# GpSimd takes the clamps of the first layer and eight scalings, two row tiles for the scatter, and new ranks

## The chip, the cores and the metric

The kernel runs on one core of a Trainium2 chip, as one program. The metric is the device time of an execution in microseconds (us), and of several executions the median. A core has five engines that each work through a list of instructions of their own, in the order in which the program was built, and wait for each other by semaphores: TensorE (PE: matrix products; PEld is its loading of weights), VectorE (DVE), ScalarE (ACT), GpSimd (POOL) and SyncE (SP, which here only starts transfers).

## The reference: what is computed

Three parts in a row, over B = 2 batches of S = 576 tokens (T = 1152 tokens), with 8 heads of 64 columns, so 512 columns a token:

```python
scores = q @ k.T / sqrt(64)                    # each batch and head: 576 x 576
kth    = the 32nd largest score of each row    # scores under it are masked
attn   = exp(scores - max); attn /= attn.sum() + 1e-9
x      = attn @ v                              # all heads of a token side by side: 512 columns
h      = x @ w_in                              # 512 -> 2048
x      = (h * cos(h)) @ w_out                  # 2048 -> 512
e      = argmax(x @ w_gate)                    # one of 8 experts for each token
gate   = softmax(x @ w_gate)[e]
out    = gate * relu(x_slot @ w1[e]) @ w2[e]   # 512 -> 1024 -> 512, at most 288 tokens an expert
```

w_in and w_out come as 64-bit floats and are turned into 32-bit floats on the chip.

## The kernel before

**Attention.** There are 36 steps; a step holds 2 x 128 rows of 576 scores (two heads of one tile of 128 tokens). `scores` makes them on PE (L482) and ACT copies them out of PSUM into `Sp` (L494). DVE finds the 32nd largest value in `pair_chain`: it takes the larger and then the smaller of the two halves of each row (L509, 128x576 in one instruction) and runs lists of maxima over them (MAX8, L513, L522, L524, and MATCH_REPLACE8, L517). `softmax` then makes the penalty on ACT (L556), subtracts it on POOL (L559), takes the exponential on ACT (L561) and divides each row by its sum: a multiplication by the reciprocal `sm`, on ACT (L570) for the first `na` steps and on DVE (L574) for the others. `products` turns the probabilities over on PE (L589), copies them on ACT (L591) and multiplies by v on PE (L603, L605; L616, L618), into `av`.

**The 2048-wide layer.** Nine tiles of 128 tokens are taken one alone and then in four pairs. `layer_in` makes 128x512 of h per unit (four tokens' blocks of w_in columns for the lone tile, two for a pair): three products of rounded halves for a pair (L684 to L686), a copy on ACT (L691) into `hs`, and a clamp of the angle into `ur` (L695, a minimum and a maximum with two constants, 36 of them for the whole kernel). `cosine` is on ACT (L712), where a switch between the exponential and the sine loads a table; `product` is on POOL (L720) and `layer_out` on PE (L729), into `x2`. `w_in` and `w_out` are converted first: `convert` makes each of 32 weight tiles of 128x512 with ACT, DVE and POOL (L389 to L408), `split_w` rounds w_in (`wh`, L365) and subtracts (`wl`, L359).

**Routing and experts.** `route` copies a tile's 128 rows into the row tile `xr` (L742), turns them over (L660, L744), makes the logits (L748) and picks the expert with small DVE instructions (L751 to L761); `place` counts the place in the expert (L786, L789 to L792) and POOL scatters the rows of `xr` to `xs` in DRAM by an indirect transfer (L795). There is one `xr`. When all nine tiles are scattered, SP reads the rows back by expert (`xg`, L953 to L957), and eight experts follow, each a first layer (L979, L981) and a second (L1010).

**What sets the order.** Every operation is entered into `Plan` with an engine, a cost and a rank. `emit` walks through time with these costs: of the operations that an engine could start within 0.02 us of its earliest, it takes the one of lowest rank. It gives buffers as they come free. The order of each engine's list thus comes out of the costs, the ranks and the rings of buffers. The parameters of the ranks and of the division of work stand in `PRM`; `FULL` is for a second pass that these inputs don't take.

```python
PRM = dict(na=22, mul=1, c0=-4.505, c1=0.411, c2=-30.35, ...)
            if s < prm["na"]:                               # scaling of step s: on ACT, else on DVE
    ring("xr", "mx", [128, RW], F32)                        # the row tile: one buffer
            P.op("dve", 0.34, lambda: DVE.tensor_scalar(angle(), T[kh], QUARTER, -QUARTER, op0=OP.min, op1=OP.max),
```

Of the kernel before, what the change touches and what calls it, by code (L numbers as in the profile page):

```python
# [7 lines left out]
F32 = mybir.dt.float32  # L8
# [4 lines left out]
AF = mybir.ActivationFunctionType  # L13
OP = mybir.AluOpType
# [3 lines left out]
B, H, S, D = 2, 8, 576, 64  # L18
HS = S // 2
T = B * S  # L20
# [5 lines left out]
RW = 520  # L26
# [14 lines left out]
QUARTER = 1.5707  # L41
FEWER = 1023.4


PRM = dict(na=22, mul=1, c0=-4.505, c1=0.411, c2=-30.35, c3=1.14, sm=-6.538, pr=0.274, sc=2.931, mx=-1.055, co=1.204, lo=5.261, ro=7.18, tb=9.729, ga=4.016, lod=10, pc=0, lv=11.745, sw=6.214, s1=0.597)
FULL = dict(na=12, mul=8, c0=3.627, c1=-2.562, c2=3.854, c3=0.425, sm=1.002, pr=3.858, sc=5.283, mx=0.736, co=8.685, lo=1.174, ro=7.507, tb=11.194, ga=4.52, lod=4, pc=0, lv=2.808, sw=1.416, s1=0.894)


class Plan:
# [202 lines left out]
def forward(ctx, lasting, tc, kq, vn, vs_, w_in, w_out, w_gate, w1, w2, out, paired):  # L252
# [3 lines left out]
    P = Plan(prm["tb"])  # L256
# [14 lines left out]
    def ring(name, pool, shape, dtype, bufs=1, tag=None, gate=None):  # L271
        P.ring(name, lambda: pools[pool], shape, dtype, bufs, tag, gate)
# [97 lines left out]
    def convert(n):  # L370

        kt = (("wt", "wt3", "wt2", "wt", "wt3", "wt2")[n % 6], n)
        kr = ("wraw2" if n % 3 else "wraw", n)
        kf = slot_of(n)
        if n < 16:
            u, kc = divmod(n, 4)
            src, r0, c0 = w_in, kc * 128, u * 512
        else:
            src, r0, c0 = w_out, (n - 16) * 128, 0

        def full():
            return T[kf] if n < 16 else T["wo", 0][:, n - 16, :]

        def bits(t):
            return t.bitcast(I32)

        last = P.dma(0.45, 1.65, lambda: SP.dma_start(
            T[kr], src[r0:r0 + 128, 2 * c0:2 * c0 + 1024].rearrange("p (n t) -> p n t", t=2)), w=[kr])
        P.op("act", 0.56, lambda: ACT.activation(T[kt], T[kr][:, :, 1].bitcast(F32), AF.Copy, scale=2.0 ** -112),  # L389
             r=[kr], w=[kt])  # L390
        if n < prm["mul"]:

            P.op("dve", 0.34, port=True, fn=lambda: DVE.tensor_scalar(bits(full()), bits(T[kt]), 3, None,
                                                                      op0=OP.logical_shift_left), r=[kt], w=[kf])
            P.op("dve", 0.60, port=True, fn=lambda: DVE.scalar_tensor_tensor(
                bits(full()), T[kr][:, :, 0], 29, bits(full()), op0=OP.logical_shift_right, op1=OP.bitwise_or),
                r=[kr], w=[kf])
            P.op("dve", 0.60, port=True, fn=lambda: DVE.scalar_tensor_tensor(
                bits(full()), bits(T[kt]), SIGN, bits(full()), op0=OP.bitwise_and, op1=OP.bitwise_or),
                r=[kt], w=[kf])  # L400
        else:
            P.op("act", 0.56, lambda: ACT.activation(full(), T[kr][:, :, 1].bitcast(F32), AF.Sign), r=[kr], w=[kf])
            P.op("dve", 0.34, port=True, fn=lambda: DVE.tensor_scalar(bits(T[kt]), bits(T[kt]), 3, None,
                                                                      op0=OP.logical_shift_left), w=[kt])
            P.op("dve", 0.60, port=True, fn=lambda: DVE.scalar_tensor_tensor(  # L405
                bits(T[kt]), T[kr][:, :, 0], 29, bits(T[kt]), op0=OP.logical_shift_right,
                op1=OP.bitwise_or), r=[kr], w=[kt])
            P.op("pool", 1.27, lambda: POOL.tensor_tensor(out=full(), in0=T[kt], in1=full(), op=OP.mult), r=[kt],  # L408
                 w=[kf])
        return last  # L410
# [133 lines left out]
    def softmax(s):  # L544
        both = [("W", s, 0), ("W", s, 1)]

        def scalars():
            w = T["W", s]
            POOL.tensor_tensor(out=T["tb", s], in0=w[:, :, TH:49:48 - TH], in1=factors[:, None, :].to_broadcast([128, 2, 2]),  # L549
                               op=OP.mult)  # L550
            if paired:
                POOL.tensor_tensor(out=edge[:, s], in0=w[:, :, 39], in1=w[:, :, TH], op=OP.subtract)
        P.op("pool", 0.3, scalars, r=both + [("halfpi",)], w=[("edge", s), ("tb", s)])
        for i in range(2):
            ks, kp = ("Sp", s, i), ("pen", (s, i))
            P.op("act", 0.67, lambda i=i, kp=kp: ACT.activation(T[kp], T["Sp", s][:, i, :], AF.Relu, scale=-BIG,  # L556
                                                                bias=T["tb", s][:, i, 0:1]), r=[ks, ("tb", s)], w=[kp])

            P.op("pool", 1.34, lambda i=i, kp=kp: POOL.tensor_tensor(  # L559
                out=T["Sp", s][:, i, :], in0=T["Sp", s][:, i, :], in1=T[kp], op=OP.subtract), r=[kp], w=[ks])  # L560
            P.op("act", 0.76, lambda i=i: ACT.activation(  # L561
                T["Sp", s][:, i, :], T["Sp", s][:, i, :], AF.Exp, bias=T["tb", s][:, i, 1:2],
                accum_out=T["sm", s][:, i:i + 1]), r=[("tb", s)], w=[ks, ("sm", s, i)], table="exp")
        P.op("pool", 0.25, lambda: POOL.tensor_scalar(T["sm", s][:, 2:4], T["sm", s][:, 0:2], 1e-9, 1.0, op0=OP.add,
                                                      op1=OP.mult), r=[("sm", s, 0), ("sm", s, 1)], w=[("sm", s, 2)])
        P.op("dve", 0.08, lambda: DVE.reciprocal(T["sm", s][:, 0:2], T["sm", s][:, 2:4]), r=[("sm", s, 2)],
             w=[("sm", s, 3)])
        for i in range(2):
            if s < prm["na"]:
                P.op("act", 0.67, lambda i=i: ACT.activation(T["Sp", s][:, i, :], T["Sp", s][:, i, :], AF.Copy,  # L570
                                                             scale=T["sm", s][:, i:i + 1]),
                     r=[("sm", s, 3)], w=[("Sp", s, i)])
                continue
            P.op("dve", 0.39, lambda i=i: DVE.tensor_scalar(T["Sp", s][:, i, :], T["Sp", s][:, i, :],  # L574
                                                            T["sm", s][:, i:i + 1], None, op0=OP.mult),
                 r=[("sm", s, 3)], w=[("Sp", s, i)], port=True)
# [75 lines left out]
    ring("ur", "mx", [128, 2, 512], F32, 2, tag="ur")  # L652
    ring("nn", "mx", [128, 512], F32)
    ring("gT", "mx", [128, 512], F32)
    ring("xr", "mx", [128, RW], F32)
    ring("xr4", "mx", [128, RW], F32, tag="raw")

    def transposes(kp, src):
# [3 lines left out]
    def layer_in(t, u):  # L662
# [29 lines left out]
        def angle():  # L692
            return T["ur", (t, u // 2)][:, u % 2]
        if paired:
            P.op("dve", 0.34, lambda: DVE.tensor_scalar(angle(), T[kh], QUARTER, -QUARTER, op0=OP.min, op1=OP.max),  # L695
                 r=[kh], w=[ku], port=True)
            return
        P.op("pool", 0.59, lambda: POOL.tensor_scalar(angle(), T[kh], INV_2PI, 0.25, op0=OP.mult, op1=OP.add), r=[kh],
             w=[ku])
# [437 lines left out]
```

## Time and profile before

| | us |
|---|---|
| median of 3 runs | 698.27 (697.89 to 698.58) |
| the profiled execution | 697.17 |
| its span, first to last instruction | 695.4 |

The span falls into three stretches. Up to about 411 us DVE works through the lists of the 36 steps. From there to 501 us PE does what is left of the 2048-wide layer. From 501 to 530 us the last two tiles are routed and read back, and from 530 us on the experts run. A row of a profile gives busy time; the time between instructions on an engine that another engine sets costs nothing by itself, so each stretch is read by the engine that has no gaps in it. The records of one engine overlap a little where instructions follow closely.

### The profile page before, as it was taken

The page shows a single profiled execution, that of the slowest core. Times are in us where ns is not written, and L with a number is a line of the kernel's source. Part 1 is how long each engine was busy: PE and PEld are TensorE (multiplying, and loading weights), DVE is VectorE, ACT ScalarE, POOL GpSimd, SP SyncE. Part 2 cuts the span into 40 slices and gives each one's busy share as a digit, 9 for nine tenths or more (in the row PEclk, how much of TensorE's full clock was granted, in tenths as well). Part 3 has the DMA queues.
Part 4 walks back from the last instruction along what each step waited for, and adds up shares of the span by engine and source line. Part 5 has one row for each costly group of instructions (what it writes and reads, how often), then busy time and mean ns, then how long its engine had stood idle before and what let it go on. Part 6 is the DMA issues. An engine that isn't in the chain of part 4 may idle for free.

```text
span 695.4 us, 11074 instructions
## 1 busy us (share of the span) xinstructions
PE 587.0 (84%) x3611; PEld 431.9 (62%) x3611; DVE 552.0 (79%) x1654; ACT 494.3 (71%) x1004; POOL 265.8 (38%) x316
## 2 busy tenths in 40 slices
PE   3333577799999999989999899999926999999994
PEld 1122355545776755866756567667425888999993
DVE  5999999999999999999999962555223888889630
ACT  4676998999799989787877764566313777778631
POOL 3466675677445545464544541322110101101111
PEclk9995658999899999999999999999956999999997
DMA  9543552064131201000000002353113677787300
GB/s 348 189 151 124 163 168 92 1 231 182 56 101 39 71 6 39 20 16 17 1 1 1 0 17 87 126 169 135 61 46 123 224 250 251 266 269 259 108 18 16
DMA packets 30786, 77.28 MB, mean 111 GB/s; under 512 B 4606, under 2 KB 4606, under 8 KB 30720
## 3 DMA queue, kind: packets, MB, share of 16 engines
q1 hardware_dynamic: 28976, 71.73, 30.7%
q0 software_dynamic: 1744, 4.76, 1.8%
q8 instruction: 30, 0.49, 0.3%
q14 instruction: 36, 0.29, 0.1%
HBM read 64.57 MB, written 12.69 MB: 111 GB/s over the span
## 4 chain that ended last, share of the span: by engine, by line
PE 40%; DVE 35%; ACT 15%; DMA 3%; issue 3%; POOL 1%; SPq 1%; POOLq 0%; DVEq 0%; ACTq 0%
PE yp L1010 11%; DVE W L513 9%; DVE C L517 8%; PE x L729 8%; PE hp L979 7%; DVE C L509 5%; PE hp L981 3%; ACT Sp L561 2%; DVE W L522 2%; ACT pen L556 2%; DVE wt L405 2%; ACT Sp L570 2%; ACT Sp L494 2%; PE h L684 2%; DVE Sp L574 2%
## 5 line engine op out<-in xcount | busy, mean ns | idle before, releaser
L729 PE MATMUL x<-wo,hs 128*128 128x512 f32 x288 | 138.2, 603 | 0.0
L559 POOL TENSOR_TENSOR Sp<-Sp,pen 128x576 f32<-128x576 f32 x72 | 98.9, 1373 | 63.9 <-ACT pen L556 63.3
L513 DVE MAX8 W<-C 128x8 f32<-128x288 f32 x288 | 118.2, 446 | 0.6
L946 DVE TENSOR_TENSOR wl<-raw,wh 128x512 fp32r<-128x512 f32 x128 | 89.9, 739 | 35.4 <-ACT wh L944 34.9
L517 DVE MATCH_REPLACE8 C<-W,C 128x288 f32<-128x288 f32 x216 | 93.8, 440 | 0.0
L589 PE MATMUL pt<-ident,Sp 128*128 128x128 f32 x324 | 56.4, 304 | 39.1 <-ACT Sp L570 32.5
L482 PE MATMUL S<-kq 64*128 64x288 f32 x256 | 57.8, 533 | 28.7 <-ACT Sp L494 19.8
L589 PEld LDWEIGHTS pt<-ident,Sp 128*128 128x128 f32 x324 | 40.0, 153 | 66.9 <-ACT Sp L570 42.1
L944 ACT ACTIVATE wh<-raw 128x512 fp32r<-128x512 f32 x128 | 74.0, 621 | 9.9 <-DMA raw<-in_w_dram 6.9
L684 PE MATMUL h<-xh,wh 128*128 128x256 f32 x256 | 78.1, 305 | 0.5 <-ACT hs L691 0.4
L979 PE MATMUL hp<-xgs,wh 128*128 128x384 f32 x256 | 76.3, 368 | 0.0
L729 PEld LDWEIGHTS x<-wo,hs 128*128 128x128 f32 x288 | 49.0, 190 | 43.5 <-issue 42.7
L1016 POOL DMA_INDIRECT out_dram<-ot,ti x16 | 16.6, 1035 | 152.8 <-ACT ot L1025 121.6
L685 PE MATMUL h<-xl,wh 128*128 128x256 f32 x256 | 71.9, 281 | 0.0
L686 PE MATMUL h<-xh,wl 128*128 128x256 f32 x256 | 71.8, 281 | 0.0
L1010 PE MATMUL yp<-wh,hc 128*128 128x512 f32 x192 | 68.4, 400 | 0.0
L509 DVE TENSOR_TENSOR C<-Sp 128x576 f32<-128x576 f32 x72 | 65.1, 904 | 3.0 <-ACT Sp L494 2.2
L720 POOL TENSOR_TENSOR hs<-hs,ur 128x512 f32<-128x512 f32 x36 | 48.4, 1356 | 46.4 <-ACT ur L712 45.0
L561 ACT ACTIVATE Sp<-Sp,tb 128x576 f32<-128x576 f32 x72 | 55.6, 773 | 14.2 <-POOL Sp L559 14.0
L981 PE MATMUL hp<-xgs,wl 128*128 128x192 f32 x256 | 65.3, 255 | 0.0
L556 ACT ACTIVATE pen<-Sp,tb 128x576 bf16<-128x576 f32 x72 | 55.2, 767 | 6.3 <-POOL tb L549 5.5
L591 ACT ACTIVATE PT<-pt 128x384 f32<-128x384 f32 x108 | 48.6, 483 | 12.2 <-PE pt L589 12.0
(138 smaller groups left out, 1365.8 us busy)
## 6 DMA issues: line engine op xcount, KB each, us to landing
raw<-in_w_dram SPq DMA_DIRECT2D x64, 512.0 KB, 3.8
wraw<-in_w_out_dram SPq DMA_DIRECT2D x16, 512.0 KB, 3.8
wraw<-in_w_in_dram SPq DMA_DIRECT2D x16, 512.0 KB, 4.0
xs<-z SPq DMA_DIRECT2D x1, 4680.0 KB
kq<-in_kq_dram SPq DMA_DIRECT2D x8, 576.0 KB, 5.7
v<-in_vn_dram SPq DMA_DIRECT2D x8, 320.0 KB, 6.2
v<-in_vs_dram SPq DMA_DIRECT2D x8, 320.0 KB, 3.3
out_dram<-z SPq DMA_DIRECT2D x1, 2304.0 KB
```

Of the source, the lines that this page charges most:

```text
L509: DVE.tensor_tensor(out=T["C", s], in0=x[:, :, 0:HS], in1=x[:, :, HS:S], op=op)
L513: P.op("dve", 0.365, lambda r=r, i=i: DVE.max(T["W", s][:, i, LIST[r]:LIST[r] + 8], T["C", s][:, i, :]), r=[("C", s, i)], w=[("W", s, i)])
L517: P.op("dve", 0.42, lambda r=r, i=i: DVE.match_replace(T["C", s][:, i, :], T["W", s][:, i, LIST[r]:LIST[r] + 8], T["C", s][:, i, :], NEG), ...
L559: P.op("pool", 1.34, lambda i=i, kp=kp: POOL.tensor_tensor(out=T["Sp", s][:, i, :], in0=T["Sp", s][:, i, :], in1=T[kp], op=OP.subtract), r ...
L589: PE.transpose(T[kp][:, c * 128:(c + 1) * 128], P2[:, cc * 128:(cc + 1) * 128], ident)
L684: PE.matmul(o, hi, a, start=(kc == 0), stop=False, skip_group_check=True)
L729: P.op("pe", 0.86, lambda f=f, a=a: PE.matmul(T["x2", t], T[kh][:, a:a + 128], T["wo", 0][:, f, :], start=(f == 0), stop=(f == 15)), r=[kh ...
L944: P.op("act", 0.52, lambda a=a, hi=hi: ACT.activation(T[hi], T[kr][:, a * 512:(a + 1) * 512], AF.Copy), r=[kr], w=[hi])
L946: P.op("dve", 0.6, lambda a=a, hi=hi, lo=lo: DVE.tensor_tensor(out=T[lo], in0=T[kr][:, a * 512:(a + 1) * 512], in1=T[hi], op=OP.subtract), ...
L979: PE.matmul(T[kp][:, 0:2 * MAIN], T[ka][:, c:c + 128], x.rearrange("p a n -> p (a n)"), start=(kc == 0), stop=False, skip_group_check=True)
L981: PE.matmul(T[kp][:, 0:MAIN], T[kb][:, c:c + 128], x[:, 0], start=False, stop=(kc == 3), skip_group_check=True)
L1010: PE.matmul(T[kp], x, w, start=(fc + n == 0), stop=(fc == 7 and n == len(uses) - 1))
```

## The change

- **Clamps.** `layer_in` puts the clamp on POOL for the first `cl` tiles in their order. With `cl=16` these are all: 36 TENSOR_SCALAR of 128x512 go from DVE to POOL.
- **Scalings of probabilities.** `na` goes from 22 to 32: steps 22 to 31 move from DVE to ACT (20 instructions). The next `np=10` steps, of which there are four (32 to 35), go to POOL as a product of `Sp` and the reciprocal spread over the row (8 TENSOR_TENSOR of 128x576). DVE has none of its 28 left.
- **Row tiles.** `xr` gets a second buffer.
- **Weights.** `mul` goes from 1 to 3: two more tiles of w_in are put together by three DVE instructions, where before DVE had two, ACT took a sign and POOL multiplied. `lod` 10 to 16: all 16 subtractions of `split_w` are on DVE (six were on POOL). `pc` 0 to 8: eight of the 16 roundings go from ACT to POOL.
- **Ranks.** All numbers of `PRM` are new, so the order of every engine differs. w_in is now converted from its last tile to its first and ahead of the last five tiles of w_out; SP's list changes in the same way (the 16 loads of w_in and the last five of w_out trade places), the rest of it is the same. ACT's list has 27 table loads, before 31. `ts=0` leaves a new branch in `convert` unused.

```diff
-PRM = dict(na=22, mul=1, c0=-4.505, c1=0.411, c2=-30.35, c3=1.14, sm=-6.538, pr=0.274, sc=2.931, mx=-1.055, co=1.204, lo=5.261, ...
+PRM = dict(np=10, cl=16, ts=0, na=32, mul=3, c0=-6.12, c1=-0.119, c2=-35.561, c3=2.753, sm=-13.198, pr=-0.47, sc=3.501, ...
...
@@ softmax
+            if s < prm["na"] + prm["np"]:
+                P.op("pool", 1.34, lambda i=i: POOL.tensor_tensor(
+                    out=T["Sp", s][:, i, :], in0=T["Sp", s][:, i, :],
+                    in1=T["sm", s][:, i:i + 1].to_broadcast([128, S]), op=OP.mult), r=[("sm", s, 3)], w=[("Sp", s, i)])
+                continue
...
-    ring("xr", "mx", [128, RW], F32)
+    ring("xr", "mx", [128, RW], F32, 2)
...
@@ layer_in
-            P.op("dve", 0.34, lambda: DVE.tensor_scalar(angle(), T[kh], QUARTER, -QUARTER, op0=OP.min, op1=OP.max),
-                 r=[kh], w=[ku], port=True)
+            on_pool = order.index(t) < prm["cl"]
+            P.op("pool" if on_pool else "dve", 0.59 if on_pool else 0.34, lambda: (POOL if on_pool else DVE).tensor_scalar(
+                angle(), T[kh], QUARTER, -QUARTER, op0=OP.min, op1=OP.max), r=[kh], w=[ku], port=True)
```

Three places in the order. First DVE's list at the end of step 25's chain and the start of the next (`Sp` scaled by `sm`, `ur` the clamped angle, `C` and `W` the lists). Before:

```order
L517 MATCH_REPLACE C<-W,C 128x288 x2
L634 TENSOR_TENSOR xl<-av,xh 64x2x64 x2
L513 MAX W<-C 128x8 x2
L509 TENSOR_TENSOR C<-Sp 128x576
L522 MAX W<-C 128x8
L566 RECIPROCAL sm<-sm 128x2
L522 MAX W<-C 128x8
L574 TENSOR_SCALAR Sp<-Sp,sm 128x576 x2
L524 MAX W<-W 128x8 x2
L509 TENSOR_TENSOR C<-Sp 128x576
L695 TENSOR_SCALAR ur<-hs 128x512
```

The same place in the list of the changed kernel, in which lines stand up to ten further down:

```order
L517 MAX W<-C 128x8 x2
L513 TENSOR_TENSOR C<-Sp 128x576
L526 MAX W<-C 128x8 x2
L570 RECIPROCAL sm<-sm 128x2
L528 MAX W<-W 128x8 x2
L513 TENSOR_TENSOR C<-Sp 128x576
L517 MAX W<-C 128x8 x2
```

The two scalings and the clamp are gone from it; the chain itself is the same.

Second ACT's list in the same stretch of the changed kernel (`pen` the penalty, `PT` the copied probabilities):

```order
L565 ACTIVATE Sp,sm<-Sp,tb 128x576
L498 ACTIVATE Sp<-S 128x2x288
L574 ACTIVATE Sp<-Sp,sm 128x576 x2
L700 ACTIVATE hs<-h 128x512
L560 ACTIVATE pen<-Sp,tb 128x576
L650 ACTIVATE xh<-av 128x128
L722 ACT_TABLE_LOAD
L722 ACTIVATE ur,turns<-ur,halfpi 128x1024
```

Each step from 22 to 31 has such a pair of scalings (L574) here, which in the list before end with step 21.

Third ACT's list at the last two tiles, with the buffers' numbers (`xr` the row tile, `gT` the rows turned over, `small` the exponentials of the logits). Before, and below it after:

```order
L742 ACTIVATE xr_4963<-x2_4675 128x512
L744 ACTIVATE gT_4969<-pt_4968 128x512
L768 ACTIVATE small_87<-small_87 128x8
L742 ACTIVATE xr_5005<-x2_4754 128x512
L744 ACTIVATE gT_5010<-pt_5009 128x512
L768 ACTIVATE small_87<-small_87 128x8
L967 ACTIVATE xgs_5107<-xp_5101 128x192
```

```order
L752 ACTIVATE xr_4961<-x2_4667 128x512
L752 ACTIVATE xr_4972<-x2_4745 128x512
L754 ACTIVATE gT_4967<-pt_4966 128x512
L754 ACTIVATE gT_4989<-pt_4988 128x512
L778 ACTIVATE small_87<-small_87 128x8 x2
L977 ACTIVATE xgs_5105<-xp_5099 128x192
```

The two tiles' copies stood one whole routing apart; now they stand next to each other, and so do their later steps.

On PE, behind the last product of step 35 with v, the list before still has 3 x 72 products of `layer_in` and 53 of `layer_out`; the changed list has 3 x 80 and 56.

## Rows read from the trace of the kernel before

**Rows 1.** Windows: stretch, its length, busy time and count of each engine, clock, transfers.
```profile
70.00:105.00 35.00, 23.71 (x132) 17.28 (x133) 34.58 (x86) 33.84 (x67) 24.93 (x23) 0.65 0.51 163
140.00:268.00 128.00, 122.61 (x822) 79.69 (x818) 123.04 (x398) 117.11 (x224) 72.61 (x88) 0.97 0.27 94
268.00:374.00 106.00, 102.27 (x709) 70.35 (x707) 103.67 (x336) 82.71 (x161) 49.95 (x66) 1.00 0.05 15
374.00:411.00 37.00, 33.68 (x228) 24.85 (x228) 35.83 (x124) 26.24 (x51) 17.74 (x26) 1.00 0.03 9
411.00:501.00 90.00, 89.73 (x473) 58.31 (x472) 38.81 (x84) 49.31 (x87) 23.50 (x24) 1.00 0.33 112
501.00:530.00 29.00, 9.04 (x69) 6.84 (x68) 5.78 (x41) 3.54 (x10) 3.21 (x5) 0.55 0.28 94
530.00:695.00 165.00, 156.34 (x889) 141.06 (x888) 113.12 (x331) 106.56 (x269) 16.56 (x16) 0.97 0.53 176
```
**Rows 2.** Timeline of DVE and PE: ends of chains 22, 32, 35; last product with v.
```profile
267.67 0.30 DVE L524 MAX8 W<-W 128x8 f32<-128x16 f32 x2
...
374.06 0.23 DVE L524 MAX8 W<-W 128x8 f32<-128x16 f32 x2
...
410.41 0.24 DVE L524 MAX8 W<-W 128x8 f32<-128x16 f32 x2
...
425.50 0.27 PE L605 MATMUL av<-PT,v 128*64 128x128 f32 x1
```
**Rows 3.** Groups by line and shape: busy us, mean ns, idle before and its releasers.
```profile
L559 POOL TENSOR_TENSOR Sp<-Sp,pen 128x576 f32<-128x576 f32 x72 | 98.9, 1373 | 63.9 <-ACT pen L556 63.3 <-DVE wt L403 0.3
L509 DVE TENSOR_TENSOR C<-Sp 128x576 f32<-128x576 f32 x72 | 65.1, 904 | 3.0 <-ACT Sp L494 2.2
L570 ACT ACTIVATE Sp<-Sp,sm 128x576 f32<-128x576 f32 x44 | 31.6, 767 | 9.3 <-DVE sm L566 9.2
L405 DVE SCALAR_TENSOR_TENSOR wt<-wraw,wt 128x512 int32<-128x512 int32 x31 | 22.4, 735 | 0.1
L695 DVE TENSOR_SCALAR ur<-hs 128x512 f32<-128x512 f32 x36 | 20.0, 555 | 6.8 <-ACT hs L691 6.7
L574 DVE TENSOR_SCALAR Sp<-Sp,sm 128x576 f32<-128x576 f32 x28 | 15.4, 591 | 0.0
L755 DVE TENSOR_SCALAR onehot<-iota,small 128x8 bf16<-128x8 f32 x9 | 5.3, 586 | 0.3
L359 DVE TENSOR_TENSOR wl<-ws,wh 128x512 fp32r<-128x512 f32 x10 | 7.8, 787 | 0.0
L334 POOL MEMSET z<- 128x520 f32 x1 | 0.5, 532 | 0.0
```
**Rows 4.** Source view of two DVE lines: shortest, median and longest in ns.
```profile
L695 DVE TENSOR_SCALAR ur<-hs x36: 407/422/1808, 127.1 to 488.2; 128x512 f32<-128x512 f32 x36
L509 DVE TENSOR_TENSOR C<-Sp x72: 736/751/1861, 12.8 to 407.5; 128x576 f32<-128x576 f32 x72
```
**Rows 5.** Timeline of PE: two products of the first layer, 21 starts apart.
```profile
427.74 0.28 PE L685 MATMUL h<-xl,wh 128*128 128x256 f32 x1
...
430.25 0.28 PE L685 MATMUL h<-xl,wh 128*128 128x256 f32 x1
```
**Rows 6.** The chain that ended last: start us, us, what.
```profile
413.52 1.72 PE x L729 x4
...
506.76 2.81 DMA xs<-xr,slot
...
512.18 1.89 PE av L748 x8
...
517.41 4.03 DMA xs<-xr,slot x2
```
**Rows 7.** Timeline of ACT and PE at the last two tiles.
```profile
502.35 1.06 PE L748 MATMUL av<-wg,gT 128*128 128x8 f32 x8 [0.75 <-ACT gT L744]
...
509.67 0.60 ACT L742 ACTIVATE xr<-x 128x512 f32<-128x512 f32 x1 [4.78 <-DMA xs<-xr,slot]
```

More of the change, by code (lines that the diff above doesn't have):

```diff
@@ L42 @@
 FEWER = 1023.4
-PRM = dict(na=22, mul=1, c0=-4.505, c1=0.411, c2=-30.35, c3=1.14, sm=-6.538, pr=0.274, sc=2.931, mx=-1.055, co=1.204, lo=5.261, ro=7.18, tb=9.729, ga=4.016, lod=10, pc=0, lv=11.745, sw=6.214, s1=0.597)
-FULL = dict(na=12, mul=8, c0=3.627, c1=-2.562, c2=3.854, c3=0.425, sm=1.002, pr=3.858, sc=5.283, mx=0.736, co=8.685, lo=1.174, ro=7.507, tb=11.194, ga=4.52, lod=4, pc=0, lv=2.808, sw=1.416, s1=0.894)
+PRM = dict(np=10, cl=16, ts=0, na=32, mul=3, c0=-6.12, c1=-0.119, c2=-35.561, c3=2.753, sm=-13.198, pr=-0.47, sc=3.501, mx=-2.942, co=16.076, lo=16.671, ro=8.401, tb=47.632, ga=7.38, lod=16, pc=8, lv=15.338, sw=11.123, s1=2.383)
+FULL = dict(np=4, cl=2, ts=0, na=12, mul=8, c0=3.627, c1=-2.562, c2=3.854, c3=0.425, sm=1.002, pr=3.858, sc=5.283, mx=0.736, co=8.685, lo=1.174, ro=7.507, tb=11.194, ga=4.52, lod=4, pc=0, lv=2.808, sw=1.416, s1=0.894)
 class Plan:
@@ L388, in convert @@
             T[kr], src[r0:r0 + 128, 2 * c0:2 * c0 + 1024].rearrange("p (n t) -> p n t", t=2)), w=[kr])
-        P.op("act", 0.56, lambda: ACT.activation(T[kt], T[kr][:, :, 1].bitcast(F32), AF.Copy, scale=2.0 ** -112),
-             r=[kr], w=[kt])
+        if n < prm["ts"]:
+            P.op("pool", 0.7, lambda: POOL.tensor_scalar(T[kt], T[kr][:, :, 1].bitcast(F32), 2.0 ** -112, 0.0, op0=OP.mult,
+                                                         op1=OP.add), r=[kr], w=[kt])
+        else:
+            P.op("act", 0.56, lambda: ACT.activation(T[kt], T[kr][:, :, 1].bitcast(F32), AF.Copy, scale=2.0 ** -112),
+                 r=[kr], w=[kt])
         if n < prm["mul"]:
```

## The prediction

> **What bounds the kernel now.** I read the windows first, with their edges put at the ends of chains, then the timeline at those edges, then the groups by line, and last the chain of waits at the end. In the windows one looks for the engine without gaps: DVE has 123.04 of 128 us from 140 to 268 us, 103.67 of 106 from 268 to 374 and 35.83 of 37 from 374 to 411 [rows 1]. So up to 411 us the pace is DVE's, and the edges are the ends of the chains of steps 22, 32 and 35 [rows 2]. From 411 to 501 us PE has 89.73 of 90 us and DVE 38.81 [rows 1]: the 2048-wide layer has fallen behind, and PE works it off. PE is nearly full before that too, 102.27 of 106 and 33.68 of 37 us, which limits what a faster DVE can give. From 501 to 530 us no engine is busy; there the chain of waits goes from one tile's scatter to the next tile's logits and scatter [rows 6]. From 530 us PE has 156.34 of 165 us [rows 1]. The work of the experts is not changed but for some earlier transposes, and I leave it at zero; what hides these is that expert 0's and 1's weights are loaded well ahead in both lists.
>
> **Step 1, up to chain 22 (268 us): nothing.** DVE loses 12 clamps of 0.555 us (-6.7), gains six subtractions of 0.787 (+4.7) and a third instruction for two weights, priced as its like on L405, 2 x 0.735 (+1.5) [rows 3]. That is -0.5 us. The conversions stand in another order, but up to chain 10 and again up to chain 22 their number is about the same; a misplaced weight is two DVE instructions, so I allow 3 us either way. ACT loses eight roundings here, which is no gain where DVE sets the pace. The moved loads of w_in and w_out are queued on SP as before, ahead of nothing that is late.
>
> **Step 2, chains 23 to 32 (106 us): -4 us.** DVE loses 18 scalings of 0.591 and nine clamps of 0.555: 10.6 + 5.0 = 15.6 us [rows 3], which would leave it 88. But ACT takes 20 scalings of 0.767, 15.3 us [rows 3], on top of its 82.7: 98.0 us of work [rows 1]. ACT becomes the bound. With no gap at all it needs 98 us (-8); at the share it has from 140 to 268 us, 117.11 of 128 or 91.5%, it needs 107 (+1); at the fullest stretch of the trace, 33.84 of 35 or 96.7%, 101.4 [rows 1]. I take 102, near the last, since ACT would now be what the others wait for, as it nearly was there. What queues behind a scaling on ACT are the copies of scores that DVE's next chain needs.
>
> **Step 3, chains 33 to 35 (37 us): -7 us.** DVE loses eight scalings (4.7), four clamps (2.2) and the one-hot comparisons of two route picks that now stand behind chain 35 (2 x 0.586, with small neighbours not counted) [rows 3]: 8.1 us, so 27.7 of work. ACT gets no scaling here, and has 26.24 of 37. POOL gets them: eight products, bounded by its other two-input instruction of that shape, 1.373 [rows 3], so 11.0 on top of 17.74 [rows 1]. That is 28.7; with waits I take 30.
>
> **Clamps on POOL.** The trace has no such instruction on POOL. The nearest rows are a memset of 128x520 at 0.532 and the two-input 1.373 [rows 3]; I take 0.6, since a clamp reads one tensor, not two. 36 of them are 22 to 49 us on an engine that has gaps in every stretch (49.95 of 106, 23.50 of 90 [rows 1]), so they lie beside other work. The cover is gone if POOL stands in line behind a penalty that ACT is late with: L559 waited 63.3 us for ACT in all [rows 3], and a clamp behind it waits with it, then the cosine and PE's L729. Units wait in four buffers of `hs`, so I put this at zero, with 0 to 3 us.
>
> POOL also makes DVE wait. The two-input L509 takes 0.751 us as its median but 0.904 as its mean and 1.861 at most; the clamp L695 0.422, 0.555 and 1.808 [rows 3, 4]. 72 x 0.153 is 11 us that L509 loses now. From 140 to 411 us POOL is busy 72.61 + 49.95 + 17.74 = 140 us [rows 1]; some 30 instructions ahead of chain 35 add 23, a sixth. If the loss grows with POOL's busy time, the 11 us become 13: two us against the change, inside the 3 us above. The Trainium skill ("GPSIMD Engine Reference", Specifications and 4.1 Engine selection) speaks against the change: the two engines share their way into SBUF, so that DVE's instructions with two SBUF inputs or in a two-port mode contend with POOL's, and elementwise work on a tile belongs on VectorE. The trace agrees, with L509's 1.861 beside its 0.751 [rows 4]; at its worst this is the third rival below.
>
> **Step 4, what PE has left: +5.4 us.** Chain 35 ends 4 + 7 = 11 us earlier, and with it the last product with v, now 15 us behind it at 425.5 [rows 2]. Behind that product PE has 24 more products of the first layer and three more of the second. The first start 2.51/21 = 0.12 us apart [rows 5], 2.9 us; the second, two rows each in the trace, are 1.72/2 = 0.86 [rows 6], 2.6 us. So PE's stretch ends 11 - 5.4 = 5.6 us earlier, 495.4 instead of 501. PE must be able to take it: from 268 to 411 us it has 135.95 busy of 143, so 7 us of gaps (its records overlap, so there is somewhat more room). 5.6 fits.
>
> **Step 5, the last two tiles: -8.1 us.** The second tile's copy waited 4.78 us for the scatter to let go of `xr` and ran at 509.67 [rows 7], 10 us after the first. With two buffers it runs as soon as its sum is there, at about 501. Its turned rows must wait for the one `gT` until the first tile's logits have read it, which end at 502.35 + 1.06 = 503.4 [rows 7]; the copy into gT is 0.6 us, so the second logits can start at about 504.1. From logits to scatter it took 517.41 - 512.18 = 5.2 us [rows 6]: 509.3 instead of 517.4, 8.1 us. What is late next is the pair of scatters themselves, which took 4.03 us to land [rows 6] and stay. Bounds: 0, if something else holds the second tile, and 9.6, if it follows right behind the first scatter at 506.76 + 1.04.
>
> **Sum.** 5.6 + 8.1 = 13.7 us. The profiled execution took 697.17 us, of which 1.8 lie around the span; it would take 683.5. The median of the runs shown is 1.1 above it, so I forecast 684.6 us.
>
> **Rivals.**
> - *DVE stays the bound all the way.* ACT and PE keep up without gaps of their own: 15.6 + 8.1 = 23.7 us earlier, minus 5.4, plus 8.1, in all 26.4 us: 671.9. For it: DVE's gaplessness now. Against: ACT's 98 us in a stretch that would be 90 long, and PE's 7 us of gaps.
> - *ACT swallows the attention's gain.* At 91.5% step 2 gives +1, and step 3's gain goes into catching up; chain 35 ends where it did, PE has 5.4 more, the routing gives 8.1: -2.7, 695.6. For it: no long stretch of the trace has ACT over 92%.
> - *The port takes more than it gives (slower).* Each of the 24 clamps and six scalings that POOL does ahead of chain 35 stops a DVE instruction for up to 1.861 - 0.751 = 1.11 us [rows 4], 33 us, against 23.7 saved: chain 35 is 10 us later, PE 5.4 more, the routing 8.1 less: 705.6. It decides from a mean wait of about 0.88 us (26.4/30). Against: now the mean loss is 0.15 us an L509.
> - *The second row tile does nothing,* since another buffer or POOL's list holds the second tile: 692.7. Against: its copy names the scatter as releaser [rows 7].
>
> **How the numbers follow.** Forecast 0.47 (its own range 679 to 690, from 102 us in step 2 going to 98 or 107); DVE all the way 0.15; ACT swallows it 0.22; the port 0.07; the row tile does nothing 0.09. The range of 8 in 10 goes from 673, above the middle of the second case, to 696, which takes in the third and fifth. About 0.2%, 1.4 us, is what a measurement of this kernel tells from no change: faster 0.87, the same 0.05 (the far end of the third case), slower 0.08.
>
> **What would show it.** Right: no scaling or clamp on DVE between 268 and 400 us; chain 32 ends near 370 us and ACT's share there is over 93%; chain 35 ends near 400; PE full from about 405 to 495; the two copies into `xr` within 2 us of each other and the last scatters some 8 us after the first tile's logits begin. Wrong: ACT with gaps and DVE still full (the second case, lower time); a mean of L509 over 1.1 us, or clamps on POOL over 1.4 (the port); PE with gaps after its last v product, which would mean that POOL's clamps are late for the cosine.

## The result and the profile after

The changed kernel takes 677.58 us (median of 4 runs, 676.42 to 678.55) where the kernel before took 698.14 beside it: a ratio of 0.9704 [0.9687, 0.9721]. The forecast was 684.6 with 673 to 696. The profiled execution took 677.23 us, of a span of 675.4, so 19.9 us less than the profiled one before. Cut at the events that the prediction used, these are:

| us | before | after | difference | forecast |
|---|---|---|---|---|
| chain 22 ends | 268.0 | 256.8 | -11.2 | 0 (±3) |
| chains 23 to 32 | 106.3 | 94.4 | -11.9 | -4 |
| chains 33 to 35 | 36.3 | 28.4 | -7.9 | -7 |
| chain 35 to the last v product | 15.2 | 25.7 | +10.5 | 0 |
| from there to the last product of the layer | 75.4 | 82.5 | +7.1 | +5.4 |
| from there to the first read of the slots | 20.5 | 13.9 | -6.6 | -8.1 |
| from there to the end | 173.7 | 173.7 | 0 | 0 |

The windows after, in the columns of [rows 1] and the stretches of its rows 2 to 6:

```profile
140.00:268.00 128.00, 124.42 (x828) 79.83 (x826) 124.28 (x402) 115.91 (x223) 76.12 (x97) 1.00 0.25 84
268.00:374.00 106.00, 104.68 (x754) 74.28 (x752) 101.23 (x346) 97.32 (x188) 62.71 (x83) 1.00 0.03 9
374.00:411.00 37.00, 37.00 (x252) 26.89 (x247) 11.45 (x47) 24.45 (x48) 22.17 (x28) 1.00 0.10 37
411.00:501.00 90.00, 80.92 (x419) 53.16 (x417) 35.21 (x103) 37.98 (x70) 26.38 (x33) 0.95 0.33 109
501.00:530.00 29.00, 23.12 (x114) 20.47 (x115) 13.60 (x44) 13.01 (x36) 0.97 (x1) 0.76 0.47 146
```

From 374 to 411 us DVE has hardly anything left (11.45 of 37 us, 35.83 before) and PE has no gap. In the timeline the ends of chains 22, 32 and 35 and the last product with v, which answer to [rows 2]:

```profile
256.53 0.29 DVE L528 MAX8 W<-W 128x8 f32<-128x16 f32 x2
...
350.99 0.25 DVE L528 MAX8 W<-W 128x8 f32<-128x16 f32 x2
...
379.42 0.16 DVE L528 MAX8 W<-W 128x8 f32<-128x16 f32 x1
...
405.04 0.27 PE L614 MATMUL av<-PT,v 128*64 128x128 f32 x1
```

Windows with the edges at these ends and at the last product of the layer (487.8), after:

```profile
256.80:351.20 94.40, 92.41 (x651) 64.42 (x650) 90.85 (x311) 87.95 (x172) 53.19 (x73) 1.00 0.05 17
351.20:379.60 28.40, 28.40 (x182) 18.41 (x183) 25.77 (x86) 24.64 (x47) 19.54 (x26) 1.00 0.00 1
379.60:405.30 25.70, 25.70 (x199) 19.60 (x197) 5.34 (x27) 15.02 (x31) 15.42 (x21) 1.00 0.03 12
405.30:487.80 82.50, 80.93 (x394) 52.54 (x393) 31.67 (x68) 39.54 (x69) 25.97 (x33) 1.00 0.37 122
```

and the last three of these stretches in the kernel before:

```profile
374.30:410.60 36.30, 33.28 (x228) 24.85 (x228) 35.49 (x120) 26.21 (x50) 17.47 (x24) 1.00 0.03 9
410.60:425.80 15.20, 14.93 (x114) 9.90 (x112) 2.08 (x7) 9.39 (x19) 5.61 (x7) 1.00 0.00 1
425.80:501.20 75.40, 75.40 (x362) 48.61 (x363) 36.78 (x78) 39.95 (x68) 18.16 (x18) 1.00 0.39 133
```

Behind chain 35, PE now has 199 + 394 = 593 instructions, before 114 + 362 = 476; between chains 32 and 35 it has 182, before 228. So a part of PE's work moved from ahead of chain 35 to behind it. That is the price of the earlier chains: 31.0 us were won at chain 35, and 17.6 of them went into PE's work that is left behind it.

PE's account says the same from its own side. Up to the last product of the layer it was busy 421.8 us and idle 79.4 before (windows added up), and is busy 418.2 and idle 69.6 after. Of the 9.8 us of idle time that went, 5.5 went before chain 9 ended, 0.5 between chains 9 and 22 and 5.1 between chains 22 and 35 (7.1 to 2.0); behind chain 35 1.3 came back. The other 3.6 of the 13.4 us are less busy time. Between chains 22 and 35 PE had 7.1 us of gaps to give; with the same work for PE, a faster DVE could not have brought the last product forward by more there.

Groups by line and shape after (busy us, mean ns, idle before):

```profile
L563 POOL TENSOR_TENSOR Sp<-Sp,pen 128x576 f32<-128x576 f32 x72 | 111.4, 1547 | 54.8 <-ACT pen L560 53.9
L513 DVE TENSOR_TENSOR C<-Sp 128x576 f32<-128x576 f32 x72 | 62.5, 868 | 4.1 <-ACT Sp L498 3.3
L574 ACT ACTIVATE Sp<-Sp,sm 128x576 f32<-128x576 f32 x64 | 46.0, 768 | 10.4 <-DVE sm L570 8.9 <-DVE W L528 1.3
L705 POOL TENSOR_SCALAR ur<-hs 128x512 f32<-128x512 f32 x36 | 23.2, 646 | 40.8 <-ACT hs L700 40.6
L579 POOL TENSOR_TENSOR Sp<-Sp,sm 128x576 f32<-128x576 f32 x8 | 9.5, 1210 | 0.6 <-DVE W L528 0.3 <-DVE sm L570 0.3
```

A clamp on POOL takes 0.646 us (0.6 taken), a scaling there 1.210 (1.373). The two-input L513 is shorter than L509 of [rows 3], 0.868 us instead of 0.904, where the prediction's 13 us of loss would make it 0.93; L563 on the other side became longer, 1.547 instead of 1.373.

The end of the routing, in the timeline after, answers to [rows 7]:

```profile
486.10 0.60 ACT L752 ACTIVATE xr<-x 128x512 f32<-128x512 f32 x1 [8.79 <-PE x L739]
487.82 0.60 ACT L752 ACTIVATE xr<-x 128x512 f32<-128x512 f32 x1 [1.12 <-PE x L739]
488.97 1.06 PE L758 MATMUL av<-wg,gT 128*128 128x8 f32 x8 [0.75 <-ACT gT L754]
...
490.61 0.60 ACT L754 ACTIVATE gT<-pt 128x512 f32<-128x512 f32 x1 [1.70 <-PE pt L669]
...
492.23 1.85 PE L758 MATMUL av<-wg,gT 128*128 128x8 f32 x8 [0.60 <-DVE small L799]
...
498.72 0.98 POOL L805 DMA_INDIRECT xs<-xr,slot  x1 [0.30 <-issue]
501.73 0.33 SPq L963 DMA_DIRECT2D xg<-xs  x1
```

The copies stand 1.7 us apart, 10 before. But the second logits begin 3.3 us after the first: the second tile's turned rows are copied only by 491.2 us, since PE turns them behind the first logits, and then the logits wait until DVE's L799 has read the first tile's count. Logits and counts share the one PSUM tile `av`.

### The profile page after: what moved, and what is told of

It reads as the page before. It is cut to its first block, busy times and chain, and to the rows that moved or that the text cites. A ratio compares the mean times of both kernels' runs of the same rounds, so it can differ in the third digit from the quotient of the medians.

```text
span 675.4 us, 11022 instructions
## 1 busy us (share of the span) xinstructions
PE 583.1 (86%) x3611; PEld 428.4 (63%) x3611; DVE 517.2 (77%) x1598; ACT 493.8 (73%) x1010; POOL 301.6 (45%) x360
## 4 chain that ended last, share of the span: by engine, by line
PE 45%; DVE 28%; ACT 16%; issue 4%; DMA 3%; POOL 2%; SPq 1%; POOLq 0%; DVEq 0%; ACTq 0%
PE yp L1020 11%; PE x L739 9%; DVE W L517 8%; DVE C L521 7%; PE hp L989 7%; DVE C L513 4%; PE hp L991 3%; ACT Sp L574 3%; PE h L693 2%; PE S L486 2%; PE h L694 2%; PE h L695 2%; ACT Sp L565 2%; ACT pen L560 2%; PE pt L598 2%
## 5 line engine op out<-in xcount | busy, mean ns | idle before, releaser
L563 POOL TENSOR_TENSOR Sp<-Sp,pen 128x576 f32<-128x576 f32 x72 | 111.4, 1547 | 54.8 <-ACT pen L560 53.9
L598 PE MATMUL pt<-ident,Sp 128*128 128x128 f32 x324 | 56.0, 298 | 25.0 <-ACT Sp L574 22.1
L513 DVE TENSOR_TENSOR C<-Sp 128x576 f32<-128x576 f32 x72 | 62.5, 868 | 4.1 <-ACT Sp L498 3.3
L565 ACT ACTIVATE Sp<-Sp,tb 128x576 f32<-128x576 f32 x72 | 55.8, 775 | 13.1 <-POOL Sp L563 12.7
L486 PEld LDWEIGHTS S<-kq 64*128 64x128 f32 x256 | 22.5, 215 | 57.5 <-ACT Sp L498 40.5
L730 POOL TENSOR_TENSOR hs<-hs,ur 128x512 f32<-128x512 f32 x36 | 46.9, 1317 | 22.3 <-ACT ur L722 20.1
```

Of the source, the lines that this page charges most:

```text
L486: PE.matmul(T[kp][:, a, 0:HS], t[p, 1, j * 128:(j + 1) * 128], t[p, 0, i * HS:(i + 1) * HS], start=True, stop=True)
L513: DVE.tensor_tensor(out=T["C", s], in0=x[:, :, 0:HS], in1=x[:, :, HS:S], op=op)
L563: P.op("pool", 1.34, lambda i=i, kp=kp: POOL.tensor_tensor(out=T["Sp", s][:, i, :], in0=T["Sp", s][:, i, :], in1=T[kp], op=OP.subtract), r ...
L598: PE.transpose(T[kp][:, c * 128:(c + 1) * 128], P2[:, cc * 128:(cc + 1) * 128], ident)
```

## The experiments

Where a kernel keeps the order of another, its lists are written out, so that no rank is found anew. The table has the ends of chains and of the layer's last product, the stretch from that to the first read of the slots (routing), and the medians, in us:

| | ch. 9 | ch. 22 | ch. 32 | ch. 35 | last product | routing | median |
|---|---|---|---|---|---|---|---|
| before | 140.8 | 268.0 | 374.3 | 410.6 | 501.2 | 20.5 | 698.14 |
| after | 131.2 | 256.8 | 351.2 | 379.6 | 487.8 | 13.9 | 677.58 |
| k0_same_order | 134.6 | 260.3 | 354.7 | 383.0 | 491.2 | 13.9 | 679.54 |
| f1_clamps_dve | 136.9 | 262.8 | 357.9 | 386.0 | 494.9 | 13.1 | 682.56 |
| f2_scalings_dve | 135.1 | 261.5 | 363.1 | 391.9 | 498.9 | 13.4 | 686.42 |
| f3_weights_old | 135.2 | 265.9 | 360.3 | 388.7 | 496.9 | 13.3 | 685.69 |
| g1_one_row_tile | 135.3 | 261.8 | 366.4 | 397.1 | 499.5 | 20.6 | 694.42 |
| g2_before_two_tiles | 141.6 | 267.6 | 375.6 | 411.7 | 503.0 | 13.8 | 691.88 |
| h1_old_ranks | 145.8 | 271.2 | 372.0 | 404.0 | 504.5 | 13.9 | 692.52 |
| h2_old_division | 135.4 | 271.2 | 374.7 | 402.8 | 502.2 | 13.8 | 691.09 |
| j1_old_order | 144.6 | 272.3 | 376.9 | 412.9 | 504.8 | 20.6 | 699.93 |
| p1_pe_less | 135.3 | 261.6 | 356.0 | 384.3 | 492.5 | 13.3 | 680.10 |
| p2_act_less | 135.3 | 261.0 | 353.7 | 381.9 | 490.1 | 13.3 | 677.65 |
| k1_tail | 135.2 | 261.5 | 355.9 | 384.3 | 492.5 | 11.6 | 677.73 |

**Parts undone in the changed kernel's order.** First the clamps back on DVE:

```diff
-PRM = dict(..., cl=16, ...)      # the order of after, written out
+PRM = dict(..., cl=0, ...)
```

> The changed kernel with its order kept operation by operation, but the 36 clamps back on DVE. If the time was saved because DVE lost them: 25 clamps of about 0.5 us stand ahead of chain 35 again, chain 35 ends 11 to 15 us later than the 379.6 of the changed kernel, and since PE lagged there by 10 us more than before, the whole is 2 to 6 us slower than 677.6. If POOL's clamps cost DVE more by waits than they save: L513's mean falls from 0.868 to under 0.8 and the time is 677 or less.

682.56 us, 0.9779 [0.9757, 0.98] of before. Chain 35 is 6.4 us later than in after, and only 3.0 later than in the kernel of the same lists (k0, below); 11 to 15 were expected. Chain 9 is 2.3 us later than in k0: between chains 8 and 9 two clamps stand on DVE, with 2.5 us. From there every stretch up to the layer's last product is within 0.8 us of k0's, although 21 more clamps stand on DVE up to chain 35, with 10.9 us. In chains 23 to 32 DVE's busy time is 92.06 us, 90.83 in k0:

```profile
262.80:357.90 95.10, 92.90 (x654) 64.75 (x654) 92.06 (x319) 88.39 (x173) 48.81 (x65) 1.00 0.05 17
```

L513's mean fell to 0.831 us (0.861 in k0), so a part of what DVE gains by giving a clamp to POOL it loses again in its other instructions. In this order the clamps' place is worth 2 to 3 us, little more than the 2.0 us between the medians of two programs with the same lists.

```diff
-PRM = dict(np=10, ..., na=32, ...)
+PRM = dict(np=0, ..., na=22, ...)
```

> The changed kernel with its order kept operation by operation, but all 28 scalings of steps 22 to 35 on DVE as before. If DVE sets the pace from chain 22 on: chain 35 ends 11 to 15 us later and the whole is 3 to 7 us slower than 677.6. If ACT became the bound there (93% busy from chain 22 to 32): ACT's relief pays for DVE's load, chain 35 ends less than 5 us later and the time is within 2 us of 677.6.

686.42 us, 0.9823 [0.9798, 0.9847]. Chains 23 to 32 take 101.6 us instead of 94.4, and DVE's busy time there is 99.56; chains 33 to 35 take 28.8 instead of 28.3. Beside k0 (679.54) the scalings' move is worth 7 us.

```diff
-PRM = dict(..., lod=16, pc=8, ...)
+PRM = dict(..., lod=10, pc=0, ...)
```

> The changed kernel with its order kept operation by operation, but the six subtractions of w_in back on POOL and the eight roundings back on ACT. The 11 us by which chain 22 ended earlier were forecast as zero. If these moves made them: chain 9 or chain 22 ends 5 us or more later than 131.2 and 256.8. If the order and DVE's fewer waits made them: chain 9 ends as it did, chain 22 ends up to 4 us earlier (six subtractions of 0.67 fewer on DVE), and the time is within 2 us of 677.6.

685.69 us, 0.9828 [0.9803, 0.9853]. Chains 10 to 22 take 130.7 us instead of 125.7, though DVE has less to do there. The window of that stretch, first with the subtractions and roundings back, then in k0:

```profile
135.20:265.90 130.70, 123.29 (x823) 79.61 (x820) 119.59 (x389) 119.04 (x226) 80.53 (x97) 0.99 0.26 92
```

```profile
134.60:260.30 125.70, 120.89 (x823) 79.22 (x820) 122.55 (x395) 114.88 (x218) 77.92 (x99) 1.00 0.27 95
```

DVE loses 3 us of work and gains 8 of gaps: it waits for POOL's L568, which scales the row sums, for 5.5 us (0.3 in k0), and for ACT's copies L650 for 3.7 (1.1). Six subtractions are back on POOL and eight roundings back on ACT (119.04 us instead of 114.88). Both were undone together, so the share of each isn't shown. The prediction put ACT's eight roundings at no gain.

**The row tile, with it out and alone.**

```diff
-    ring("xr", "mx", [128, RW], F32, 2)
+    ring("xr", "mx", [128, RW], F32)
```

> The changed kernel with one row tile, planned anew. If the second tile gave what the traces show between the last product of the layer and the first read of xg (20.7 us before, 13.9 after): 6 to 8 us slower than 677.6. If the routes would have overlapped anyway, or something else holds the second tile: within 2 us.

694.42 us, 0.995 [0.993, 0.997]. The routing is 6.6 us longer than after's. The rest is another order, which the planner made anew for one buffer and in which chains 23 to 35 take 135.3 us instead of 122.8, and chain 9, which is 4.1 us later, as in k0 (3.4). So this run isn't the price of a buffer alone. The other way round is nearly clean (its last product is 1.8 us later), the kernel before with the second buffer:

```diff
-    ring("xr", "mx", [128, RW], F32)
+    ring("xr", "mx", [128, RW], F32, 2)
```

> The kernel before with a second row tile and nothing else, planned anew. If the gain of the second tile stands by itself: 6 to 8 us under 698.1. If it needs the new ranks: within 2 us of 698.1.

691.88 us, 0.9894 [0.9863, 0.9926]: 7.2 us less than the kernel before beside it, and the routing is 6.7 us shorter. All kernels with one row tile have 20.5 or 20.6 us there, all with two and the one `av` 13.1 to 13.9. The rival "the second row tile does nothing" is out.

**Division of work against ranks.** The changed kernel with all ranks of before, then with the division of before:

```diff
-PRM = dict(np=10, cl=16, na=32, mul=3, lod=16, pc=8, c0=-6.12, c1=-0.119, ...)
+PRM = dict(np=10, cl=16, na=32, mul=3, lod=16, pc=8, c0=-4.505, c1=0.411, ...)
```

> The changed kernel (new division of work, two row tiles) with the ranks of before, planned anew. If the division and the tile make the gain: 678 to 684. If the ranks make the attention's part of it: 688 to 693, the row tile's 7 us alone.

692.52 us, 0.9903 [0.9865, 0.9941].

```diff
-PRM = dict(np=10, cl=16, na=32, mul=3, lod=16, pc=8, c0=-6.12, ...)
+PRM = dict(np=0, cl=0, na=22, mul=1, lod=10, pc=0, c0=-6.12, ...)
```

> The changed kernel's ranks and two row tiles, with clamps, scalings and weights divided as before, planned anew. If the division makes the attention's gain: 688 to 693. If the ranks make it: 678 to 684.

691.09 us, 0.9888 [0.9849, 0.9927]. Neither is faster than the row tile alone, which both have (g2, 691.88), by more than 0.8 us. h2 has chain 9 at 135.4, so of the 6.2 us that k0 wins up to there 5.4 come with the ranks. Up to chain 9 DVE has fewer clamps (two instead of four) and subtractions (two instead of six), since they now stand further on. Chains 33 to 35 are as short in h2 as in k0 (28.3 us), with clamps and scalings on DVE:

```profile
374.70:402.80 28.10, 28.10 (x197) 19.83 (x194) 27.89 (x95) 23.18 (x44) 13.87 (x21) 1.00 0.01 2
```

With the ranks goes also what DVE loses beside POOL. L513, which halves the rows of scores, with the ranks of before (h1) and with the new ones (h2); its mean is 0.893 us with the old ranks and the old division (g2) and 0.861 with both new (k0):

```profile
L513 DVE TENSOR_TENSOR C<-Sp 128x576 f32<-128x576 f32 x72 | 65.4, 908 | 7.4 <-ACT Sp L498 6.4
```

```profile
L513 DVE TENSOR_TENSOR C<-Sp 128x576 f32<-128x576 f32 x72 | 59.4, 825 | 3.5 <-ACT Sp L498 2.9
```

h1 has chain 35 at 404.0, 6.6 us before its time, and its last product 3.3 us late: PE has 100.5 us behind chain 35, 90.6 before. The last of these keeps the written order of before, with one row tile and the new division but for `mul`, which stays at 1:

```diff
-PRM = dict(na=22, mul=1, ...)    # the order of before, written out
+PRM = dict(np=10, cl=16, na=32, mul=1, lod=16, pc=8, ...)
```

> The order of before kept operation by operation and one row tile, but clamps on POOL, steps 22 to 31 scaled on ACT and 32 to 35 on POOL, all subtractions of w_in on DVE and eight roundings on POOL. If the division makes the gain without any new order: chain 35 ends 15 to 25 us earlier than 410.6, but PE's list is the old one, so 8 to 13 us under 698.1. If the new order is needed: no more than 4 us under 698.1.

699.93 us, 1.0019 [0.9997, 1.004]: nothing. Of the 20.6 us between the medians, the row tile gives 7 by itself, and 2 belong to no edit (k0, below); the other 11 or 12 need division and ranks together. Which of the ranks it takes isn't shown.

**The same lists once more.** Another program with the same list on every engine:

> The changed kernel again, every engine's instructions in the same order, as another program. In the kernels with one part undone, chain 9 ended at 135.1 to 136.9 us, although their instructions up to there are the changed kernel's, which ends it at 131.2. Theory A: the 131.2 belongs to this order of instructions, and the edits disturb it. Then chain 9 ends at 131 to 132 us here and the time is 676.4 to 678.6. Theory B: which engine wins the port (or when the clock rises) differs from program to program. Then chain 9 may end near 135 to 137 us here, TensorE's granted clock from 90 to 110 us is 0.50 instead of 0.74 and 0.66, and the time is 681 to 683: some 4 us of the gain would belong to no edit.

679.54 us (678.71 to 680.93), 0.9731 [0.97, 0.9762]. Chain 9 ends at 134.6, so 3.4 us of the 9.6 that after wins up to there belong to no edit; in every other kernel of this order it is 134.6 to 136.9 too. Behind chain 9 every stretch up to the first read of the slots agrees within 0.1 us; from there k0 is 2.0 us shorter (171.7 instead of 173.7), which I haven't explained. TensorE's granted clock from 90 to 110 us, as a share of 2.4 GHz, is lower in k0 (0.67 and 0.50 instead of 0.74 and 0.66), but it isn't what DVE waits for: between chains 4 and 9 DVE has 0.8 us of gaps in both kernels, and 2.9 us more of busy time in k0 (62.30 instead of 59.41). The timeline shows where, first after, then k0 (`wt` is a weight on its way to 32 bits):

```profile
77.35 0.41 DVE L407 TENSOR_SCALAR wt<-wt 128x512 int32<-128x512 int32 x1
79.62 1.30 DVE L409 SCALAR_TENSOR_TENSOR wt<-wraw,wt 128x512 int32<-128x512 int32 x2
80.82 0.82 DVE L526 MAX8 W<-C 128x8 f32<-128x288 f32 x2
...
77.62 4.43 POOL L563 TENSOR_TENSOR Sp<-Sp,pen 128x576 f32<-128x576 f32 x1 [0.26 <-ACT pen L560]
```

```profile
77.73 1.51 DVE L407 TENSOR_SCALAR wt<-wt 128x512 int32<-128x512 int32 x1
...
77.68 1.27 POOL L563 TENSOR_TENSOR Sp<-Sp,pen 128x576 f32<-128x576 f32 x1
```

In k0 POOL starts 0.05 us ahead, and DVE's shift takes 1.51 us instead of 0.41. After has DVE 0.27 us ahead; POOL's subtraction lasts until 82.05, that is 1.23 us from the moment at which DVE's run of shifts and two-input instructions is over and MAX8 begins (80.82). Here whoever is first keeps the other out, DVE for as long as such instructions follow each other (seven of them from 77.35 us on). The Trainium skill says so ("SBUF — State Buffer", Who interferes with whom): the engine that issues first gets the shared ports for its whole instruction, and the other is blocked, not slowed. The trace agrees in the waiting, with 1.51 us for DVE behind one instruction of POOL; POOL's 4.43 us span several of DVE's. A lost start costs DVE 1.1 us; a won one costs POOL 3.2, and DVE's chains don't wait for that here. In k0 five shifts between 60 and 110 us took 1.48 to 1.51 us in this way, in after one.

**Less work on PE, then on ACT, in chains 23 to 32.** Both keep the order of after. The first leaves out the smallest of a product's three parts in eight units, the second the division of each row by its sum in steps 23 to 31, so p1 computes coarser sums and p2 something else; only their times are used:

```diff
+                    two = paired and order.index(t) in (3, 4)     # layer_in
...
-                    PE.matmul(o, lo, a, start=False, stop=(kc == 3), skip_group_check=True)
+                    if not two:
+                        PE.matmul(o, lo, a, start=False, stop=(kc == 3), skip_group_check=True)
```

> The changed kernel in the same order; eight units of the first layer, which run between 277 and 349 us, leave out the third of their three products (64 of PE's products, some 0.13 us each: 8.5 us of PE's work; the layer's sums lose their smallest term). Theory 'PE is the bound' (PE has 2.0 us of gaps in all from chain 22 to chain 35): chains 32 and 35 and the last layer product end 6 to 8.5 us earlier, 669 to 671.6 us. Rival 'ACT is the bound in chains 23 to 32' (the prediction's step 2): the chains end where they did, PE has 8 us more of gaps, 676 to 677.6 us.

```diff
+            if paired and 23 <= s < 32:                            # softmax
+                P.op("act", 0.67, lambda: None, r=[("sm", s, 3)], w=[("Sp", s, i)])
+                continue
```

> The changed kernel in the same order; steps 23 to 31 leave out their 18 scalings on ACT, 18 x 0.768 = 13.8 us of ACT's work (the probabilities' turned copies are multiplied by 1/16 instead, in instructions that are there anyway, and the count of doubtful angles is switched off, so that the second pass isn't taken). Theory 'PE is the bound': chains 32 and 35 and the last layer product move by no more than PE's 2.0 us of gaps, 675.5 to 677.6 us. Rival 'ACT is the bound' (step 2): chain 32 ends 8 to 13.8 us earlier and the last layer product with it, 664 to 670 us.

p1 took 680.10 us (0.9731 [0.9701, 0.9761]), p2 677.65 (0.9691 [0.9658, 0.9723]). The windows of chains 23 to 32, in k0, with less on PE, and with less on ACT:

```profile
260.30:354.70 94.40, 92.40 (x650) 64.40 (x650) 90.83 (x310) 87.97 (x172) 53.12 (x73) 1.00 0.05 17
```

```profile
261.60:356.00 94.40, 86.02 (x587) 56.75 (x587) 90.79 (x310) 87.72 (x172) 53.02 (x73) 1.00 0.05 17
```

```profile
261.00:353.70 92.70, 91.83 (x653) 64.80 (x652) 90.29 (x310) 78.21 (x156) 52.56 (x73) 1.00 0.05 18
```

With 6.4 us less on PE the stretch is as long as it was, 94.40; my theory that PE is the bound there fell. With 9.8 us less on ACT it is 1.7 us shorter; so ACT alone isn't the bound either, and the prediction's step 2 fell with it. DVE's time is the same in all three, 90.3 to 90.8; and the window of the kernel with the scalings back on DVE grows with it:

```profile
261.50:363.10 101.60, 95.66 (x660) 65.43 (x661) 99.56 (x329) 79.62 (x158) 54.94 (x73) 1.00 0.05 16
```

DVE still sets the pace, at 96%, with PE and ACT so close behind that easing either gives 0 to 1.7 us. That DVE is the only bound isn't shown: no run took work from DVE there. In chains 33 to 35 it is PE that has no gap (28.30 of 28.30 us in k0, DVE 25.68); no run took work from PE in that stretch.

**A version that undoes the new wait.** The last tile gets its own buffer and its own PSUM bank, and its steps stand ahead of the first tile's count:

```diff
-        kp, kg, kl = ("pt", ("r", t)), ("gT", ("r", t)), ("av", ("r", t))
+        kp, kg, kl = ("pt", ("r", t)), ("nn" if t == order[-1] else "gT", ("r", t)), ("h" if t == order[-1] else "av", ("r", t))
```

> The changed kernel in the same order up to the last two tiles; there the last tile has its own buffer for its turned rows and its own PSUM bank for its logits, both idle by then, and its transposes and logits stand ahead of the first tile's count. Theory (the second logits waited for the one logits bank until VectorE had read the first tile's ranks, 492.23 instead of about 490): the second logits begin near 490 us, the last scatter near 496 instead of 498.7, 674.5 to 675.5 us. Rival (the three scatters on POOL or the landing of the first set the end): 676.5 to 677.6 us.

```profile
493.67 1.06 PE L758 MATMUL av<-wg,gT 128*128 128x8 f32 x8
...
494.59 1.04 PE L758 MATMUL h<-wg,nn 128*128 128x8 f32 x8
...
498.46 1.06 POOL L805 DMA_INDIRECT xs<-xr,slot  x1 [15.07 <-DVE small L801]
...
501.10 0.97 POOL L805 DMA_INDIRECT xs<-xr,slot  x1 [0.30 <-issue]
504.09 0.33 SPq L963 DMA_DIRECT2D xg<-xs  x1
```

The second logits follow 0.9 us behind the first, 3.3 in after, and the routing takes 11.6 us instead of 13.9. Buffer, bank and place in the list were changed together, so the share of each isn't shown. The time is 677.73 us (677.47 to 679.01), 0.9705 [0.9679, 0.9732] of before; beside k0, on the same chip, the median is 1.8 us less, and the runs of the two overlap by 0.3 us (678.71 to 680.93 there). Against after's 677.58 it wins nothing, and the 674.5 to 675.5 us that were expected from there didn't come, since its chain 9 ends at 135.2 like k0's.

## Why the prediction came out, step by step

The time lay in the range, 7.0 us under the forecast. The direction and the two sources (the chains, the routing) were right. The terms were not, and that the sum still lay in the range is in part luck, since large errors had opposite signs.

- **Step 1, "nothing", was -11.2.** Of this, 3.4 us belong to no edit (k0). The count of instructions was right: up to chain 22 DVE has 741 instructions before and 737 after, and in k0 the clamps make -6.4 us, the subtractions +4.0 and the conversions +1.0. What failed is the sentence "the 11 us become 13". Adding up what DVE's elementwise instructions took over their median in the kernel before (0.751 us for L509, 0.422 for a clamp and so on), DVE lost 33.7 us up to chain 35 before, 21.7 in k0 and 19.2 after, with POOL busy for 222, 229 and 241 us. So the loss doesn't grow with POOL's busy time. Nor does it go by how many of DVE's instructions can be caught. With the new ranks it is 22.1 us under the old division (h2) and 20.4 with the clamps back (f1); with the old ranks it is 29.0 under the new division (h1), and 29.9 in the old order (j1). It goes with the order; what in the order does it isn't shown beyond the starts that k0 shows. And the subtractions and roundings of w_in that the sum took as +4.7 us on DVE and nothing on ACT were a gain together, 5.0 us in chains 10 to 22 (f3).
- **Step 2, -4, was -11.9.** DVE lost 13.1 us of busy time (15.6 counted), and ACT did not become the bound. Its 98 us never came: the stretch holds 87.95. In its groups 18 scalings add 13.0 us, 4.4 left with a table load, a unit's copy and four copies of scores and `PT` that the new ranks put elsewhere, and 3.4 lie in records that overlap more: the groups' sum rises by 8.6 us (91.7 to 100.3), the busy time by 5.2. ACT's share is 93% all the same, as the prediction's sign for "right" had it, so that sign didn't tell the bound; DVE's 96% and p2 did. Of DVE's two terms, the scalings bear it (7.2 us in f2); the clamps, counted at 5.0, gave 0.7 (f1). The rival "DVE all the way" gave 23.7 us for chains 23 to 35, and 19.8 were measured, but it counted DVE's work for chains 33 to 35 too, where PE has no gap.
- **Step 3, -7, was -7.9, and that is luck.** Clamps and scalings went to POOL and nobody waits for them there, but they are not what made the stretch shorter: with the clamps back on DVE it takes 28.1 us (f1), with the scalings back 28.8 (f2), under the whole old division 28.1 (h2), and under the new division in the old order 36.0 (j1). The order makes it. PE has no gap there (28.40 us) and 182 instructions instead of 228, and two picks of routes, some 5 us of small DVE instructions of which the prediction counted 1.2, stand elsewhere.
- **Step 4, +5.4, was +17.6.** What failed is "and with it the last product with v": that the 15 us between the two stay. I counted PE's products behind the last v product (+7.1 us measured) and not those that the new list puts between chain 35 and that product: 199 rows instead of 114, which is in part the work that left chains 33 to 35. PE's gaps are the better measure: of the 7.1 us between chains 22 and 35, 5.1 were won.
- **Step 5, -8.1, was -6.6.** The second copy came at once, as said. The second logits were to begin 1.75 us after the first and began 3.3 after: PE turned the second tile's rows only behind the first logits, and then the shared `av` held the logits until the first tile's count was read. I had not looked for a second user of that tile. k1 gives 2.3 us of it back. From the second logits to the first read it is 9.5 us in both kernels.
- **The sum** came out better than its parts: steps 1 to 3 gave 20.0 us more than forecast, step 4 cost 12.2 more, step 5 gave 1.5 less; 6.3 remain of that (683.5 to 677.2 for the profiled execution).
- **The port rival (slower)** is out: clamps on POOL have 0.646 us, and L513's mean is 0.868, not over 1.1. In part it was right: put back on DVE, the 23 clamps up to chain 35 take 13.4 us there, but DVE's busy time grows by 5.7 only (365.0 to 370.7, f1).
- Outside all steps, 3.4 us up to chain 9 hang on the start of five instructions, not on the change.

## What to carry to other kernels

Where one engine's lists set the pace and another works off a backlog behind them, set the gain against the gaps of the second engine: here 31.0 us at the end of the lists became 13.4 at the end of the backlog. A new division of work and the order that goes with it are one change; here either alone was worth next to nothing. When a term comes out as forecast, undo that part alone before you believe its reason. When a buffer is doubled, go through every other tile on that path for a second user.

## What the hardware showed

- DVE's shift of 128x512 and POOL's subtraction of 128x576 exclude each other: 1.51 us instead of 0.41 for DVE when POOL is 0.05 us ahead, 4.43 instead of 1.27 for POOL when DVE is ahead by 0.27. Two programs with the same lists (after and k0) differ by 3.4 us at chain 9; in k0 five shifts took some 1.5 us between 60 and 110 us, in after one.
- Up to chain 35, every elementwise instruction of DVE that took over 0.15 us longer than its median in the kernel before ran beside an instruction of POOL: 40 of 40 before, 34 of 34 in k0, 31 of 31 after.
- POOL's one-input clamp of 128x512 takes 0.646 us in after, less than half of its two-input product of the same shape (L730, 1.317).
